# Two-level w_out products spread over 21 steps, three in flight, in eight PSUM banks

## The chip, the cores and the metric

The kernel runs on one core of a Trainium2 chip. A core has a matrix engine (TensorE, PE in the profile, PEld for its weight loads), VectorE (DVE), ScalarE (ACT), GpSimd (POOL) and SyncE (SP), which issues most of the transfers. Each engine works through its own instructions in order; semaphores hold it where it needs what another engine makes. TensorE writes into PSUM, eight banks of 2 KB a partition; VectorE and ScalarE read the banks. The metric is the device time of one execution in microseconds (us), less is better. Before the change the median of three runs is 871.32 us (868.98 to 872.26).

## The reference

The program is an attention block followed by a feed-forward block, all in float32 on the chip (the feed-forward weights arrive as float64).

```python
# attention: q, k, v of shape (8, 12, 448, 64)
scores = norm(q) @ norm(k).T / sqrt(64);  attn = softmax(scores);  x = attn @ v
# bridge to x of shape (3584, 768)
h = x @ w_in                       # w_in 768 x 1024
e = exp(h - max(h));  solu = h * e / (sum(e) + 1e-9)
ln = (solu - mean) / sqrt(var + 1e-6) * g_ln
out = ln @ w_out                   # w_out 1024 x 768
```

## The kernel before

The kernel goes through three stages: attention (to about 332 us of the span), the products with `w_in` (to 585.0 us) and the products with `w_out` (to the end). The diff is about the third.

**Products with fewer multiplications.** Each of the two matrix products is done in Winograd's form of Strassen's scheme: a 2 x 2 block product with 7 block multiplications in place of 8, and sums of blocks ahead and behind. For `w_out` this is done on two levels. The 3584 rows are 7 row blocks (`NS`, index n) of four tiles of 128 rows. For each n there are seven outer products P1 to P7. The outer product of a name takes one wide operand (`HALVES`: a11, a12, s2, s1, s3, s4, a22), made from the transposed activations u, and one of seven prepared weight areas. Inside it are again seven small products, called p1, p2, p6, p5, p7, p4, p3 in their order (`outer_product`, L1152 on). Each is a group of four matmuls of 128 x 128 by 128 x 192 (`mul`, L1158; the matmul is L1168).

**What a group needs and gives.** p1, p6, p7 and p4 add into one bank A, one after the other: after each, the bank is read (`plus`, L1176 on: L1180 on ScalarE for P1 and P5, L1182 on VectorE for the five others, which add a former result at once), and the next group adds into the same bank. So p6 waits for the read after p1, p7 for that after p6, p4 for that after p7. p2 has a bank C, read by VectorE (L1204); p5 and p3 share a bank B, read by VectorE after p7 (L1216, which needs the read of A after p7) and after p3 (L1224). The results of P1, P6 and P7 are kept as Q1, U2 and U3, V is the sum of P6 and P5, and C22 that of P7 and P5 (`finish`, L1235 on, one VectorE instruction of 768 columns each, L1246). Four results of each n are stored by SP (L1231).

**Operands.** u of a tile was written to DRAM in a transposed order by `ff_spread` (a VectorE transpose at L1061, four stores on SP at L1064). `load_u` (L1098) fetches a quarter of 256 KB on SP into a tile called ur. The wide operands come from these: a11, a12, a22 are ScalarE copies (`arrange`, L1116), s1 to s4 VectorE sums (L1121, L1126, L1131, L1136), each made of two instructions (two tiles t) that follow each other. `inner_sums` (L1138) makes the inner block sums with four GpSimd instructions (L1147 to L1150), one of which overwrites a quarter of the operand.

**Order.** The order is written out by hand in slots; a slot holds at most one group. `ORDERS` gives the slot in a period of 49 (one n) at which each outer product begins, and its groups take every second slot from there. So two outer products are in flight, and their groups alternate. `unit` issues the group with all that it entails, and `when(slot, f)` hangs other work behind it: loads, sums, copies. `later(x, f)` runs f when x units have passed; one unit is four slots of this stage, or one product of the stage with `w_in`. So the last tiles' activation work (`ff_max` L1022, `ff_exp` L1028, `ff_mult` L1032, `ff_moments` L1040 on, `ff_norm` L1052, `ff_spread`) runs on inside the first 36 slots of the stage with `w_out`.

**Weight check.** The kernel's float64 conversion holds for weights in a certain range. `check_next` reads both weight matrices again in 28 pieces, every nine slots, and `check_w` (L584) takes the smallest and the largest of each piece with two VectorE reductions (L587, L588); `check_worst` and `check_all` join them with a limit on x into a flag, on which a general path would run instead.

**Memory.** Pools: `big` has tags h, u (three buffers each) and b (two), shared in turn by activations, stores of u and outer results (`big_tile`, L779). For n = 0, a11 and a12 come from a pool `first` ahead of the stage; all others from `u`, opened when the stage begins. PSUM has banks A, B and C for each of two streams and one for the check.

Of the kernel before, what the change touches and what calls it, by code (L numbers as in the profile page):

```python
# [366 lines left out]
def fast_path(  # L367
# [78 lines left out]
    def setup():  # L446
        nc.gpsimd.memset(mhalf, -0.5)
        nc.gpsimd.memset(seven, 7.0)
        nc.gpsimd.memset(eps, 1e-6)


        nc.gpsimd.memset(ones, 0.0)
# [131 lines left out]
    def check_w(x, raw):  # L584

        hi = raw[:, :, 1].bitcast(FP32)
        nc.vector.tensor_reduce(extent[:, 0, x : x + 1], hi, AX, OP.min, apply_absolute_value=True)  # L587
        nc.vector.tensor_reduce(extent[:, 1, x : x + 1], hi, AX, OP.max, apply_absolute_value=True)  # L588

    def check_worst():  # L590
        nc.vector.tensor_reduce(worst[:, 0:1], extent[:, 0], AX, OP.min)
        nc.vector.tensor_reduce(worst[:, 1:2], extent[:, 1], AX, OP.max)
        nc.vector.tensor_reduce(worst[:, 2:3], xmax, AX, OP.max)

    def check_all():
# [3 lines left out]
        pw = last["ps"].tile([P, 4, P], FP32, tag="w", name="pw")[0:1]  # L599
        for i in range(3):  # L600
            nc.tensor.transpose(pw[:, i], worst[:, i : i + 1], ident)
        nc.vector.tensor_reduce(one[:, 0:1], pw[:, 0], AX, OP.min)
        nc.vector.tensor_reduce(one[:, 1:3], pw[:, 1:3], AX, OP.max)
        nc.vector.tensor_scalar(one[:, 0:1], one[:, 0:1], 2.0 ** -15, None, OP.is_ge)
        nc.vector.tensor_scalar(one[:, 1:2], one[:, 1:2], 2.0, None, OP.is_lt)
        nc.vector.tensor_scalar(one[:, 2:3], one[:, 2:3], 256.0, None, OP.is_le)
        nc.vector.tensor_tensor(one[:, 0:1], one[:, 0:1], one[:, 1:2], OP.mult)
        nc.vector.tensor_tensor(one[:, 0:1], one[:, 0:1], one[:, 2:3], OP.mult)
# [489 lines left out]
    def load_u(n, t, h):  # L1098
        own = last.get("u", last["first"])
        r = us[n, "raw", t, h] = own.tile([P, P * HF], FP32, tag="raw", name="ur", bufs=2 if own is last["first"] else 8)  # L1100
# [5 lines left out]
    def operand(n, name):  # L1106
        own = last["first"] if n == 0 and name in ("a11", "a12") else last["u"]
        bufs = 2 if own is last["first"] else 8
        us[n, name] = own.tile([P, 2, HF, 4, 32], FP32, tag="op", name=name, bufs=bufs)
        return us[n, name]  # L1110

    def arrange(n, name, tile, h):

        o = operand(n, name)
        for t in range(2):
            nc.scalar.copy(o[:, t], in_turn(n, tile + t, h))  # L1116

    def sum_s1(n):
        o = operand(n, "s1")
        for t in range(2):  # L1120
            nc.vector.tensor_tensor(o[:, t], in_turn(n, 2 + t, 0), in_turn(n, 2 + t, 1), OP.add)  # L1121

    def sum_s2(n):
        o = operand(n, "s2")
        for t in range(2):
            nc.vector.tensor_tensor(o[:, t], us[n, "s1"][:, t], in_turn(n, t, 0), OP.subtract)  # L1126

    def sum_s3(n):
        o = operand(n, "s3")
        for t in range(2):  # L1130
            nc.vector.tensor_tensor(o[:, t], in_turn(n, t, 0), in_turn(n, 2 + t, 0), OP.subtract)  # L1131

    def sum_s4(n):
        o = operand(n, "s4")
        for t in range(2):
            nc.vector.tensor_tensor(o[:, t], in_turn(n, t, 1), us[n, "s2"][:, t], OP.subtract)  # L1136

    def inner_sums(n, name):  # L1138

        own = last["first"] if n == 0 and name in ("a11", "a12") else last["u"]  # L1140
        a = us[n, name]
        sm = us[n, name, "sums"] = own.tile(
            [P, 3, KC, 4, 32], FP32, tag="sums", name="sums", bufs=2 if own is last["first"] else 4
        )
        a11, a12, a21, a22 = [a[:, t, k * KC : (k + 1) * KC] for t in range(2) for k in range(2)]
        s1, s2, s4 = [sm[:, i] for i in range(3)]
# [5 lines left out]
    def outer_product(n, name, stream):  # L1152
# [5 lines left out]
        def mul(bank, a, i, begin):  # L1158
            x = us[n, operand_name]
            sm = us[n, operand_name, "sums"]  # L1160
            a = {
                "a11": x[:, 0, 0:KC], "a12": x[:, 0, KC:], "s3": x[:, 1, 0:KC], "a22": x[:, 1, KC:],
                "s1": sm[:, 0], "s2": sm[:, 1], "s4": sm[:, 2],
            }[a]
            if begin:
                k[bank] = last["ps"].tile([P, 512], FP32, tag=f"{bank}{stream}", name=bank)[:, 0:N2]
# [24 lines left out]
        def p1():  # L1191
            mul("A", "a11", 0, True)
            us[n, name] = big_tile(name)[:, 0 : 2 * HO].rearrange("p (t n) -> p t n", t=2)
            if name == "P1":
                us[n, "Q1"] = us[n, name]
            if name == "P6":
                us[n, "U2"] = us[n, name]
            if name == "P7":
                us[n, "U3"] = us[n, name]
            plus(temp("q1"), "A", 0, 0)  # L1200

        def p2():
            mul("C", "a12", 1, True)
# [435 lines left out]
```

## Time and profile before

| | before |
|---|---|
| median of 3 runs | 871.32 us |
| profiled execution | 870.22 us |
| its span | 868.3 us |
| TensorE, VectorE busy | 809.5 us, 690.8 us |
| ScalarE, GpSimd busy | 407.2 us, 449.1 us |
| matmuls of the w_out stage | 1372 of 5020 |
| stage with w_out | 585.0 us to the end |

The page is that of one execution. Busy time is the time in which an engine worked on an instruction. A row of a group of instructions has the line, the engine and operation, output and input with shapes, the count, then the busy time and the mean time of one in ns, then the idle time of the engine ahead of them with what ended it. In the table by stage, each row is a stretch of the span, each engine's busy time in it (number of instructions), the granted TensorE clock (1.00 is full), the share of the DMA engines' time and the rate. In a list of waits a row says who waited for whom, the total in us, how many times, and the longest. The chain of waits goes back from the last instruction to what released it; it is given in order of time, with start, length and what ran. The timeline gives start, length and instruction, and in brackets the idle time before it and its releaser.

### The profile page before, as it was taken

The page shows a single profiled execution, that of the slowest core. Times are in us where ns is not written, and L with a number is a line of the kernel's source. Part 1 is how long each engine was busy: PE and PEld are TensorE (multiplying, and loading weights), DVE is VectorE, ACT ScalarE, POOL GpSimd, SP SyncE. Part 2 cuts the span into 40 slices and gives each one's busy share as a digit, 9 for nine tenths or more (in the row PEclk, how much of TensorE's full clock was granted, in tenths as well). Part 3 has the DMA queues.
Part 4 walks back from the last instruction along what each step waited for, and adds up shares of the span by engine and source line. Part 5 has one row for each costly group of instructions (what it writes and reads, how often), then busy time and mean ns, then how long its engine had stood idle before and what let it go on. Part 6 is the DMA issues. An engine that isn't in the chain of part 4 may idle for free. (4 is left out here: it accounts for less than half of the span.)

```text
span 868.3 us, 14895 instructions
## 1 busy us (share of the span) xinstructions
PE 809.5 (93%) x5020; PEld 470.0 (54%) x5020; DVE 690.8 (80%) x1249; ACT 407.2 (47%) x643; POOL 449.1 (52%) x632
## 2 busy tenths in 40 slices
PE   5989999999999999999999999995798978999796
PEld 3334344343444444444444444444797978898796
DVE  5778888887988885899999998886657776776854
ACT  5677876876877862566655544331211102112010
POOL 1343464554564564222444786752755656666560
PEclk9999999999999999999999999997999999999999
DMA  5677877777767634256553454316333625456321
GB/s 115 140 170 180 188 163 176 160 158 176 169 139 173 143 102 123 74 137 191 150 146 86 123 148 118 86 48 193 92 137 126 245 84 191 137 195 218 102 72 60
DMA packets 271941, 122.27 MB, mean 141 GB/s; under 512 B 190704, under 2 KB 257264, under 8 KB 271856
## 3 DMA queue, kind: packets, MB, share of 16 engines
q1 hardware_dynamic: 257600, 111.56, 49.3%
q10 hardware_dynamic: 14256, 9.67, 4.0%
q8 instruction: 42, 0.69, 0.4%
q14 instruction: 43, 0.35, 0.1%
HBM read 84.48 MB, written 36.70 MB: 140 GB/s over the span
## 5 line engine op out<-in xcount | busy, mean ns | idle before, releaser
L968 PE MATMUL b<-w_in,xg 128*128 128x512 f32 x336 | 151.2, 592 | 0.0
L788 ACT ACTIVATE E<-s 128x896 f32<-128x896 f32 x168 | 138.9, 936 | 10.7 <-PE s L798 10.5
L798 PE MATMUL s<-qkT 64*64 64x448 f32 x1152 | 123.1, 554 | 1.4 <-DVE qkT L774 0.8
L968 PE MATMUL b<-w_in,xsum 128*128 128x512 f32 x252 | 115.0, 592 | 0.0
L851 PE MATMUL o<-E,v 128*64 128x448 f32 x576 | 113.5, 543 | 0.0
L968 PEld LDWEIGHTS b<-w_in,xg 128*128 128x128 f32 x336 | 63.8, 190 | 80.2 <-issue 77.4
L670 POOL COPY ss<-part 32x56 f32<-32x56 f32 x88 | 42.0, 477 | 102.7 <-DVE part L660 100.0
L1168 PE MATMUL A<-w_out,s 128*128 128x192 f32 x336 | 69.1, 338 | 23.6 <-DVE u L1182 21.4
L709 POOL TENSOR_TENSOR qkn<-qk,ny 128x896 f32<-128x896 f32 x46 | 77.9, 1713 | 24.1 <-DVE ny L700 10.9
L1168 PE MATMUL B<-w_out,sums 128*128 128x192 f32 x392 | 78.0, 332 | 4.6 <-DVE P L1216 4.6
L798 PEld LDWEIGHTS s<-qkT 64*64 64x64 f32 x1152 | 47.4, 164 | 62.1 <-ACT E L788 30.7
L968 PEld LDWEIGHTS b<-w_in,xsum 128*128 128x128 f32 x252 | 47.9, 190 | 60.3 <-issue 56.4
L851 PEld LDWEIGHTS o<-E,v 128*64 128x64 f32 x576 | 39.2, 137 | 72.6 <-issue 68.0
L1046 POOL TENSOR_TENSOR he<-he,mhalf 128x1 f32<-128x1 f32 x28 | 16.7, 598 | 113.9 <-DVE he L1045 113.5
L1168 PEld LDWEIGHTS A<-w_out,s 128*128 128x128 f32 x336 | 55.4, 191 | 30.8 <-DVE u L1182 23.7
L1168 PEld LDWEIGHTS B<-w_out,sums 128*128 128x128 f32 x392 | 67.4, 194 | 5.1 <-issue 5.1
L1052 ACT ACTIVATE u<-u,shift,he 128x1024 f32<-128x1024 f32 x28 | 34.7, 1239 | 66.8 <-POOL shift L1048 56.5
L1168 PE MATMUL A<-w_out,a 128*128 128x192 f32 x252 | 51.8, 337 | 10.1 <-ACT u L1180 6.0
L660 DVE TENSOR_REDUCE part<-sq 128x28 f32<-128x896 f32 x46 | 49.0, 1082 | 15.2 <-ACT sq L652 13.4
L1147 POOL TENSOR_TENSOR sums<-s 128x256 f32<-128x256 f32 x28 | 21.9, 781 | 70.4 <-PE B L1168 54.9
L1180 ACT COPY q<-A 128x192 f32<-128x192 f32 x14 | 4.5, 318 | 111.0 <-PE A L1168 111.0
L825 DVE TENSOR_TENSOR es<-E 128x896 f32<-128x896 f32 x48 | 52.6, 1097 | 0.5 <-ACT E L788 0.5
(135 smaller groups left out, 1523.4 us busy)
## 6 DMA issues: line engine op xcount, KB each, us to landing
ur<-ud SPq DMA_DIRECT2D x58, 256.0 KB, 4.8
ud<-ub SPq DMA_DIRECT2D x112, 128.0 KB, 2.6
xd<-xo SPq DMA_DIRECT2D x24, 448.0 KB, 3.7
qk<-in_q_dram SPq DMA_DIRECT2D x184, 56.0 KB, 2.3
qk<-in_k_dram SPq DMA_DIRECT2D x184, 56.0 KB, 2.1
v<-in_v_dram SPq DMA_DIRECT2D x24, 384.0 KB, 4.9
out_dram<-P SPq DMA_DIRECT2D x21, 384.0 KB, 2.7
raw<-in_moe_w_in_dram SPq DMA_DIRECT2D x12, 512.0 KB, 4.4
```

The source lines that it names most:

```text
L660: nc.vector.tensor_reduce(norms[m]["part"][:, i], st[n]["sq"], AX, OP.add)
L670: e.tensor_copy(ss[g * 32 : g * 32 + 32], part[o * 32 : o * 32 + 32])
L709: e.tensor_tensor(d["qkn"], d["qk"].rearrange("p s b d -> p (s b) d"), y.rearrange("p b -> p b ()").to_broadcast([P, 2 * NB, 32]), OP.mult,)
L788: nc.scalar.activation(d["E", kc], s[:, :, 0:S], AF.Exp)
L798: nc.tensor.matmul(s[c : c + D, h, 0:S], d["qkT"][hh, 1, keys], d["qkT"][hh, 0, :], start=True, stop=True,)
L825: nc.vector.tensor_tensor(d["es"], d["E", 0], d["E", 1], OP.add)
L851: nc.tensor.matmul(d["o"][h * D : (h + 1) * D, :], quads[n // 2]["v"][:, n % 2 * 2 + h, kc], d["E", kc][:, h], start=False, stop=(kc == NJ ...
L968: nc.tensor.matmul(o, a[:, c], w_in[i][:, c], start=(c == 0), stop=(c == HD - 1))
L1046: nc.gpsimd.tensor_tensor(e, e, mhalf, OP.pow)
L1052: nc.scalar.activation(d["u"], d["u"], AF.Identity, scale=d["e"], bias=d["shift"])
L1147: nc.gpsimd.tensor_tensor(s1, a21, a22, OP.add)
L1168: nc.tensor.matmul(k[bank], a[:, c].rearrange("p a i -> p (a i)"), w_out[:, area, i, c], start=begin and c == 0, stop=c == KC - 1, skip_gr ...
```

## The change

- **Order.** One list `ORDER` = P1, P5, P6, P2, P7, P3, P4 for all n. Outer product number q begins at slot 7q (`STEP`), and its seven groups p1, p2, p6, p5, p7, p4, p3 stand at `PLACES` 0, 4, 8, 10, 12, 16, 20 from there. So three are in flight.
- **PSUM.** A has four banks, B and C two each. The check's bank is gone; it borrows a C bank.
- **Wide sums one by one.** `make(n, name, t)` is one instruction; the two of an operand have slots of their own. s2, s3 and s4 read the copies a11, a12 where they read the loaded tiles before. V and C22 are two instructions of 384 columns each (`both`).
- **First operands.** For n = 0, a11 and s1 (was a12) are made ahead of the stage; the other five are made in slots 0 to 20.
- **Buffers.** Outer results take tags in the order h, u, h, u, h, u, b, b. Loaded quarters have six buffers (was eight), the inner sums have a fourth part in place of the overwrite.
- **Activation work.** `ff_norm` and `ff_spread` of the last two tiles run one unit earlier, `ff_spread` of all others one unit later.
- **Check.** Per piece three ScalarE instructions, three slots apart: two squares with biases and a Relu whose sum goes to `extent`; it is zero if all weights lie in the range. `check_all` takes two transposes in place of three.

```diff
     def check_w(x, raw):
-        hi = raw[:, :, 1].bitcast(FP32)
-        nc.vector.tensor_reduce(extent[:, 0, x : x + 1], hi, AX, OP.min, apply_absolute_value=True)
-        nc.vector.tensor_reduce(extent[:, 1, x : x + 1], hi, AX, OP.max, apply_absolute_value=True)
+        v = raw[:, :, 1]
+        t = last["u"].tile([P, S], FP32, tag="range", name="range", bufs=1)[:, 0 : v.shape[1]]
+        return [
+            lambda: nc.scalar.activation(t, v, AF.Square, scale=2.0 ** -30, bias=limits[:, 0:1]),
+            lambda: nc.scalar.activation(t, t, AF.Square, bias=limits[:, 1:2]),
+            lambda: nc.scalar.activation(t, t, AF.Relu, bias=limits[:, 2:3], accum_out=extent[:, x : x + 1]),
+        ]
...
-            for x, f in zip((1, 2, 3, 5, 7, 9), (ff_max, ff_exp, ff_mult, ff_moments, ff_norm, ff_spread)):
+            waits = (1, 2, 3, 5, 6, 8) if g == NG - 1 else (1, 2, 3, 5, 7, 10)
+            for x, f in zip(waits, (ff_max, ff_exp, ff_mult, ff_moments, ff_norm, ff_spread)):
...
-    ORDERS = (
-        (("P1", 0), ("P2", 9), ("P6", 14), ("P5", 23), ("P7", 28), ("P3", 37), ("P4", 42)),
-        (("P1", 2), ("P5", 7), ("P6", 16), ("P2", 21), ("P7", 30), ("P3", 35), ("P4", 44)),
-    )
-    PERIOD = 49
+    ORDER = ("P1", "P5", "P6", "P2", "P7", "P3", "P4")
+    STEP = 7
+    PLACES = (0, 4, 8, 10, 12, 16, 20)
...
+        if name == "a11":
+            nc.scalar.copy(o, in_turn(n, t, 0))
...
+        elif name == "s1":
+            nc.vector.tensor_tensor(o, in_turn(n, 2 + t, 0), in_turn(n, 2 + t, 1), OP.add)
+        elif name == "s2":
+            nc.vector.tensor_tensor(o, us[n, "s1"][:, t], us[n, "a11"][:, t], OP.subtract)
+        elif name == "s3":
+            nc.vector.tensor_tensor(o, us[n, "a11"][:, t], in_turn(n, 2 + t, 0), OP.subtract)
+        else:
+            nc.vector.tensor_tensor(o, us[n, "a12"][:, t], us[n, "s2"][:, t], OP.subtract)
...
-        nc.gpsimd.tensor_tensor(a21, a11, a21, OP.subtract)
+        nc.gpsimd.tensor_tensor(s3, a11, a21, OP.subtract)
...
-                k[bank] = last["ps"].tile([P, 512], FP32, tag=f"{bank}{stream}", name=bank)[:, 0:N2]
+                tag = f"{bank}{q % 2}" + (str(q // 2 % 2) if bank == "A" else "")
+                k[bank] = last["ps"].tile([P, 512], FP32, tag=tag, name=bank)[:, 0:N2]
...
+    def out_tile(name):
+        tag = "huhuhubb"[len(turns) % 8]
+        turns.append(tag)
...
+        nc.vector.tensor_tensor(us[n, x][:, t], us[n, "U2" if x == "V" else "U3"][:, t], us[n, "P5"][:, t], OP.add)
...
+        follow(parts, 66, lambda: early("a11", 0, (0,)))
+        follow(parts, 67, lambda: early("a11", 1, (0,)))
+        follow(parts, 72, lambda: early("s1", 2, (0, 1)))
+        follow(parts, 77, lambda: early("s1", 3, (0, 1)))
...
+                for place, f in zip(PLACES, outer_product(n, name, q)):
+                    slots[STEP * q + place] = f
...
+                if q > 1:
+                    when(STEP * q - 6, lambda n=n, x=x: inner_sums(n, x))
+            for x, t, slot in (("V", 1, 31), ("V", 0, 34), ("C22", 1, 45), ("C22", 0, 52)):
+                when(base + slot, lambda n=n, x=x, t=t: both(n, x, t))
...
+            at_load = (10, 11, 15, 16, 17, 18, 21, 22) if n == 1 else (4, 5, 8, 9, 10, 11, 16, 17)
+            blocks = (0, 0), (1, 0), (2, 0), (3, 0), (2, 1), (3, 1), (0, 1), (1, 1)
...
+            late = 6 if n == 1 else 0
+            made(n, "a11", base + 12 + late, base + 15 + late)
+            made(n, "s1", base + 21 + late, base + 24 + late)
+            made(n, "s2", base + 28 + late, base + 38)
+            made(n, "a12", base + 33, base + 36)
+            made(n, "s3", base + 40, base + 42)
+            made(n, "s4", base + 47, base + 49)
+            made(n, "a22", base + 53, base + 55)
...
+        made(0, "s2", 0, 3)
+        made(0, "s3", 6, 8)
+        made(0, "a12", 10, 11)
+        made(0, "a22", 12, 14)
+        made(0, "s4", 17, 20)
...
-            when(70 + 9 * x, lambda x=x: check_next(x))
+            when(55 + 9 * x, begin_check)
+            when(58 + 9 * x, go_on)
+            when(61 + 9 * x, go_on)
```

More of the change, by code (lines that the diff above doesn't have):

```diff
@@ L1123, in sum_s2 @@
[L1123 to L1136, printed above, removed]
+        own = last.get("u", last["first"])
@@ L1138, in inner_sums @@
     def inner_sums(n, name):
[L1140 removed]
+        own = last.get("u", last["first"])
         a = us[n, name]
         sm = us[n, name, "sums"] = own.tile(
[L1143 removed]
+            [P, 4, KC, 4, 32], FP32, tag="sums", name="sums", bufs=2 if own is last["first"] else 4
         )
         a11, a12, a21, a22 = [a[:, t, k * KC : (k + 1) * KC] for t in range(2) for k in range(2)]
[L1146 removed]
+        s1, s2, s3, s4 = [sm[:, i] for i in range(4)]
@@ new lines, in fast_path @@
+            for slot, (t, h) in zip(at_load, blocks):
+                when(base + slot, lambda n=n, t=t, h=h: load_u(n, t, h))
+            late = 6 if n == 1 else 0
[6 more added lines that the diff above has]
+            made(n, "a22", base + 53, base + 55)
@@ L1569, in check_first, with begin_check, go_on @@
                 raw[x] = load_again(x)
-        when(60, check_first)
+        when(45, check_first)
         for x in range(len(again)):
-            when(70 + 9 * x, lambda x=x: check_next(x))
-        when(PERIOD * NS - 18, check_worst)
-        when(PERIOD * NS - 12, check_all)
-        for slot in range(PERIOD * NS + 8):
+            def begin_check(x=x):
+                sets["check"] = check_w(x, raw.pop(x))
+                sets["check"].pop(0)()
+            def go_on(x=x):
+                sets["check"].pop(0)()
+                if not sets["check"] and x + 2 < len(again):
+                    raw[x + 2] = load_again(x + 2)
+            when(55 + 9 * x, begin_check)
+            when(58 + 9 * x, go_on)
+            when(61 + 9 * x, go_on)
+        end = period * NS + PLACES[-1] - STEP + 1
+        when(end - 35, check_worst)
+        when(end - 28, check_all)
+        for slot in range(end):
             if slot in slots:
```

146 lines of the change are left out of this document (60 added, 86 removed).

## The prediction

> **What bounds the kernel now.** I read the page first, then the table of busy time by stage, then the chain of waits and the timeline inside the stage that the diff touches.
>
> ```profile
> span 868.3 us, 14895 instructions
> PE 809.5 (93%) x5020; PEld 470.0 (54%) x5020; DVE 690.8 (80%) x1249; ACT 407.2 (47%) x643; POOL 449.1 (52%) x632
> PEclk9999999999999999999999999997999999999999
> ```
>
> TensorE is busy for 93% of the span, which seems to leave little. But the share hides a stage, the w_out products, that starts at 585.0 us, where the one dip of the clock row also lies. By stage (columns: length; busy PE, PEld, DVE, ACT, POOL with counts; clock; DMA share; GB/s; the row with two columns holds the w_out matmuls alone):
>
> ```profile
> 500.00:550.00 50.00, 50.00 (x118) 22.18 (x117) 44.41 (x74) 22.40 (x34) 40.08 (x44) 1.00 0.42 114
> 585.00:645.00 60.00, 43.21 (x215) 40.40 (x216) 39.45 (x79) 11.19 (x23) 28.47 (x38) 0.86 0.40 118
> 645.00:862.50 217.50, 196.35 (x1162) 186.83 (x1160) 153.29 (x367) 30.65 (x76) 120.71 (x155) 1.00 0.45 150
> ...
> 585.00:862.50 277.50, 239.23 (x1372) 227.01 (x1372) 0.97 0.44 143
> ```
>
> 1372 matmuls are 343 groups of four (7 row blocks, 7 outer products, 7 groups). What one group takes undisturbed, and what disturbs it, stands in the chain of waits:
>
> ```profile
> 654.71 0.61 DVE extent L588
> 655.32 1.39 DVE s L1121 x2
> 656.71 0.27 DVE P L1204
> 656.98 0.28 DVE u L1182
> ...
> 657.30 0.92 PE A L1168 x4
> ...
> 660.02 1.19 DVE V L1246
> ...
> 661.53 0.92 PE A L1168 x4
> ...
> 842.38 0.65 PE C L1168 x4
> ```
>
> A group costs 0.65 us, so 343 cost 223 us. The last one ends near 862.2, so the stage takes 277.2 and 54 us of it are waits and slow clock. 54 groups (35 us) fill the first 60 us, 25 over; the other 289 (188 us) fill 217, 29 over. The chain says whom TensorE waits for: VectorE, at a long instruction (a weight check, a wide sum, the sum V) ahead of a short read of a bank. Waits of the steady part, then of the start:
>
> ```profile
> PE A L1168 <- DVE u L1182: 19.6, 19, 1.8
> ...
> PE A L1168 <- ACT u L1180: 6.0, 1, 6.0
> PE B L1168 <- DVE P L1216: 4.6, 1, 4.6
> DVE V L1246 <- DMA ud<-ub: 3.5, 1, 3.5
> ```
>
> **The change, part by part.**
>
> *Three products in flight.* The bank A of a product is read four times between its groups. The shortest such cycle is in the timeline, where a product runs last and alone:
>
> ```profile
> 859.35 0.81 PE L1168 MATMUL A<-w_out,a 128*128 128x192 f32 x4
> ...
> 860.20 0.36 DVE L1182 TENSOR_TENSOR u<-A,P 128x192 f32<-128x192 f32 x1 [0.29 <-PE A L1168]
> ...
> 860.61 0.92 PE L1168 MATMUL A<-w_out,a 128*128 128x192 f32 x4 [0.45 <-DVE u L1182]
> ```
>
> From the start of p7's group to that of p4's: 860.61 - 859.35 = 1.26 us, with VectorE free. Today p7 and p4 stand two slots apart, 1.30 us when another product fills the slot between: 0.04 us to spare, so nearly any VectorE work in the way is paid by TensorE. After, p6, p7 and p4 stand four slots apart (2.60 us): 1.34 us to spare; p1 to p6 and p5 to p3 have eight. The seven places are distinct modulo 7, so from slot 14 every slot holds a group until the last product drains.
>
> *Checks to ScalarE, wide sums one by one.* VectorE's pieces (count, then min/median/max ns in the rows on ur; mean ns in the others):
>
> ```profile
> L1182 DVE TENSOR_TENSOR u<-A,P 128x192 f32<-128x192 f32 x48 | 16.9, 351 | 5.5 <-PE A L1168 5.5
> L587 DVE TENSOR_REDUCE extent<-again 128x1 f32<-128x448 f32 x26 | 15.8, 608 | 0.0
> L1246 DVE TENSOR_TENSOR V<-P,P 128x768 f32<-128x768 f32 x6 | 6.9, 1149 | 0.6
> ...
> L1121 DVE TENSOR_TENSOR s<-ur x14: 679/1196/1235, 592.2 to 804.1; 128x512 f32<-128x512 f32 x14
> L1126 DVE TENSOR_TENSOR s<-s,ur x14: 679/683/686, 595.4 to 816.9; 128x512 f32<-128x512 f32 x14
> L1136 DVE TENSOR_TENSOR s<-ur,s x14: 677/796/1214, 596.6 to 824.4; 128x512 f32<-128x512 f32 x14
> L1131 DVE TENSOR_TENSOR s<-ur x14: 677/684/1215, 600.7 to 819.1; 128x512 f32<-128x512 f32 x14
> ```
>
> The longest single piece falls from a pair (checks, two sums: 1.2 to 2.3 us) to one sum, 0.68 to 1.23 us, or half a V, about 0.57: alone, all below 1.34. A period of 49 slots is 31.9 us. In it VectorE has 41 bank reads (3 for each of P1 and P5, whose other reads are ScalarE's, 7 for each of five others), at the 0.28 that they take back to back in the chain: 11.5. Eight wide sums at the medians: 2 x (1.20 + 0.68 + 0.68 + 0.80) = 6.7. V and C22: 2.3. Together 20.5 us, 64%, where the checks (4 x 1.2) would make it 80%.
>
> What is left is bunching. In slots 38 to 54 stand one s2, two s3, two s4 and two halves of C22: 4.8 us at the medians, 6.7 at the longest, and some 14 reads, 4.0, in 11.05 us. Following the slots one by one, VectorE is at most 0.6 us late at the medians and 1.9 at the longest, so TensorE waits 0 to 0.6 us; for s1, s1, s2, V, V in slots 21 to 34, 0 to 0.4. Loads that come late add something that the rows don't give, 0 to 1 us a period. I take 1 us a period in the middle of these: 6 us for the six steady ones, bounds 0 and 12.
>
> ScalarE gets three instructions for each check. Nearest row, and landings (min/median/max) of the loads ur, then of the check's:
>
> ```profile
> L531 ACT ACTIVATE tmp<-raw,seven 128x384 f32<-128x384 uint32 x16 | 10.2, 637 | 8.4 <-DMA raw<-in_moe_w_out_dram 8.4
> ...
> DMA to landing us min/median/max: 2.6/4.8/6.9
> ...
> DMA to landing us min/median/max: 3.1/3.5/4.6
> ```
>
> Of 448 instead of 384 elements, about 0.7 us each: 28 x 2.1 = 59 us on an engine that was busy 30.65 in 217.5. Its reads for P1 and P5 stand behind single pieces of 0.7 against 1.34 to spare: nothing. Without that cover each check would cost up to 2.1.
>
> *The start.* Waits there were a bank read stuck on ScalarE behind copies whose loads had not landed (6.0), on VectorE behind the same loads (4.6), and V waiting for a buffer that a store held (3.5). The six loads no longer stand behind the stores on SP, the first copies that need them stand at slot 10, and V's buffers come from tags that the stores don't hold: these three go. Two s1 sums move into the stage before; by its row TensorE is busy all the time there and VectorE 44.4 of 50, so they fit (2.4 us if not). What stays is VectorE's own work, now denser:
>
> ```profile
> L1061 DVE STREAM_TRANSPOSE ub<-u 128x1024 f32<-128x1024 f32 x4 | 4.9, 1234 | 2.0 <-DMA ud<-ub 2.0
> L1040 DVE BATCH_NORM_STATS2 bs<-u 128x6 f32<-128x512 f32 x4 | 2.6, 680 | 0.0
> L1032 DVE TENSOR_TENSOR u<-h,u 128x1024 f32<-128x1024 f32 x2 | 2.5, 1236 | 0.0
> ```
>
> Ahead of P1's read at slot 12, VectorE has two s2 (1.4), two transposes (2.5), two products (2.5), two s3 (1.4), one pair of statistics (1.4) and two reads (0.6), and a maximum of about 1.2 left from the stage before: 11 us. P1's p3 at slot 20, 13 groups or 8.5 us in, waits for that read: 2.5 to 4 us. To slot 27 follow two transposes, a second pair of statistics and two s4; from 28 to 48 some 15 us of work stand against 13.7 us of groups. Added up, slot 49 comes 8 us later than its groups alone; bounds 4 (that first wait alone) and 16 (two thirds of today's 25).
>
> ```profile
> 589.50:595.30 5.80, 0.00 (x0) 0.00 (x0) 1.50 (x3) 1.46 (x3) 0.00 (x0) 0.73 0.87 272
> 595.30:609.00 13.70, 9.05 (x27) 8.31 (x28) 13.36 (x26) 1.74 (x3) 6.62 (x8) 0.62 0.61 186
> ...
> 624.20:629.00 4.80, 1.46 (x8) 1.16 (x8) 1.25 (x3) 0.00 (x0) 1.24 (x2) 1.00 0.46 109
> 629.00:632.60 3.60, 3.53 (x13) 3.53 (x14) 3.21 (x9) 0.00 (x0) 0.00 (x0) 0.59 0.01 2
> ```
>
> After the gaps of 5.8 and 4.8 us the granted clock was 0.62 and 0.59. A first wait of 2.5 to 4 us may or may not do it; VectorE would hide most of slow groups, so I add 1 us, bounds 0 and 6. The Trainium skill (TensorE: Matmul & The Clock Gate, "Why this matters for your kernels") sets the limit at idle gaps of about 3 us; the rows agree that 4.8 is over it, and by that rule the term lies nearer 6 than 0 and the time near 836.
>
> *The rest* (an extra sum tile instead of writing in place, one transpose fewer at the end, norms one unit later) is under 0.5 us, hidden behind 0.65 us groups. The drain of the last product: four slots between p7 and p4 hold one group of another, so 0.04 to spare as now: 0.5.
>
> **Sum.** 8 + 1 + 6 + 0.5 = 15.5 of the 54 us stay; 38.5 go. The profiled execution took 870.22 us (span 868.3), 0.13% under the median 871.32: 870.2 - 38.5 = 832.
>
> **Rivals.**
>
> *Loads too late.* s1 follows its loads by 11 slots, 7.2 us, and a11 by 8, 5.2, at landings of 4.8 in the median and 6.9 at most, now with a sixth more traffic per us (277 us of it in 239). If a11 and s1 wait 2 us each period beyond what is spare: 6 x 2 = 12, 844. For it: the small margin; against it: the median.
>
> *VectorE and GpSimd in each other's way.* The sum s1 has 679 and 1235 ns for the same shape. If every wide sum and half V takes the longer time (12 x 0.5 = 6 us a period, VectorE at 83%) about 2.5 us come through: 6 x 2.5 = 15 instead of 6, 841. GpSimd itself, 28 x 0.78 (120.71 by 155) = 22 of 31.9 us, does not bound. The Trainium skill (SBUF — State Buffer, "Who interferes with whom") has a VectorE instruction with two SBUF inputs block, or be blocked by, a GpSimd instruction that reads SBUF, whole; the doubled times agree in kind.
>
> *The start stays as it is* (VectorE bound plus slow clock): 25 instead of 9, 848.
>
> *Nothing gained* (the freed waits fall to another engine at the same rate): about 870. Against it: by the sums above no other engine is busy for over 70% of a period.
>
> *Slower: ScalarE's queue stuck behind the check loads.* A check's first instruction waits for a load issued 12 slots, 7.8 us, before, and bank reads of P1 and P5 (28 of 49 slots) queue behind it. SP holds stores for long:
>
> ```profile
> SPq L1231 <- DVE P L1224: 50.9, 15, 8.9
> ```
>
> Were each load held 8.9 us and landing in 4.6, it would be 5.7 late, 4.4 beyond what is spare, for 16 of the 28 checks: 70 us, 902. It decides from 3.8 us late (16 x 2.4 = 38.5). Against it: what stands before a load on SP was due earlier by its slot, and landings were 3.1 to 4.6.
>
> **Chances.** Forecast 60% (own range 820 to 842), late loads 11%, VectorE against GpSimd 9%, start as it is 8%, nothing gained 4%, slower 6%, and 2% faster than 820. The range 820 to 850 holds the forecast, and the three rivals that end below 850. 0.5%, 4.4 us, is about what can be told from no change here. Faster 0.90, same 0.04, slower 0.06.
>
> **What would show it.** Right: in the steady part TensorE's waits for VectorE under 8 us, not 19.6; groups at 0.65 without the 0.92 restarts; no wait of 4 us or more after the first period; checks on ScalarE and no wait of its bank reads behind them. Wrong: ScalarE or VectorE waiting for ur or the check's tile; a clock well under 1 beyond 610 us; the stage longer than 255 us.

## The result, and the profile after

The median went from 870.15 us (867.11 to 872.26, four runs) to 824.85 us (824.47 to 826.51, four runs): a ratio of 0.9486, with a 95% interval of 0.9452 to 0.9519. The forecast was 832, the range 820 to 850. The profiled execution took 826.51 us. Three rows of its page, which answer to those of before:

```profile
span 824.4 us, 14924 instructions
PE 796.2 (97%) x5019; PEld 465.7 (56%) x5019; DVE 673.0 (82%) x1203; ACT 461.3 (56%) x755; POOL 462.3 (56%) x635
PEclk9999999999999999999999999999999999999999
```

The dip of the clock is gone, and TensorE is busy for 13 us less with the same matmuls (5019 against 5020, as `check_all` has one transpose fewer), none of which runs at a low clock now. By stretches of the stage with w_out (columns as in the prediction):

```profile
586.80:620.00 33.20, 28.04 (x161) 25.93 (x162) 32.58 (x64) 10.02 (x20) 22.63 (x28) 1.00 0.44 134
620.00:818.50 198.50, 197.55 (x1215) 196.76 (x1213) 139.32 (x335) 86.50 (x192) 139.12 (x165) 1.00 0.50 169
```

From 620 us on TensorE is busy 197.55 of 198.50 us. For sizes below a microsecond I use the start of the groups. Here are the first, the 55th, the 155th and the last group after, then three of the same of before (the timeline of TensorE; start, length):

```profile
586.81 0.92 PE L1167 MATMUL A<-w_out,a 128*128 128x192 f32 x4 [0.78 <-DVE h L979]
...
629.00 0.81 PE L1167 MATMUL A<-w_out,sums 128*128 128x192 f32 x4
...
694.00 0.81 PE L1167 MATMUL A<-w_out,s 128*128 128x192 f32 x4
...
817.10 0.81 PE L1167 MATMUL B<-w_out,sums 128*128 128x192 f32 x4
```

```profile
585.01 0.92 PE L1168 MATMUL A<-w_out,a 128*128 128x192 f32 x4 [0.79 <-DVE h L975]
...
645.21 0.81 PE L1168 MATMUL C<-w_out,s 128*128 128x192 f32 x4
...
861.37 0.81 PE L1168 MATMUL B<-w_out,sums 128*128 128x192 f32 x4
```

From 629.00 to 694.00 one hundred groups start, 0.650 us each, without a break. What a stretch takes beyond 0.6505 us a group, I call idle (0.6505 is used for every kernel; with 0.650 each "rest" below would be 0.14 us more). First part, 54 groups: before 60.20 - 35.13 = 25.1 us, after 42.19 - 35.13 = 7.1. Rest, 288 groups: before 216.16 - 187.34 = 28.8, after 188.10 - 187.34 = 0.8. Together 46.1 us went; the stage began 1.8 us later (586.81 against 585.01), and the time from the start of the last group to the end grew by 0.4 us (7.3 against 7.0), so the span is 43.9 us shorter. The 1.8 us can't be told from chance: the first matmul with w_in already starts 1.8 us later (333.41 against 331.61), the diff adds only three small memsets on GpSimd ahead of it, and the kernels of the experiments began the stage anywhere between 584.8 and 589.1 us.

What TensorE, and ScalarE ahead of it, still wait for at the start (584 to 622 us), and in the second fence TensorE's waits from 622 us on; columns: total, times, longest:

```profile
ACT a L1124 <- DMA ur<-ud: 3.0, 2, 2.8
ACT u L1032 <- DVE ub L1065: 2.6, 1, 2.6
PE A L1167 <- ACT u L1179: 2.3, 2, 1.6
...
PE B L1167 <- DVE P L1211: 1.2, 1, 1.2
...
PE A L1167 <- POOL sums L1147: 0.8, 1, 0.8
```

```profile
PE A L1167 <- DVE u L1181: 0.4, 1, 0.4
```

19.6 us in 19 waits for VectorE's bank reads became 0.4 us in one.

### The profile page after: what moved, and what is told of

Read it like the earlier page. It is cut to its first block, busy times and chain, and to the rows that moved or that the text cites. A ratio compares the mean times of both kernels' runs of the same rounds, so it can differ in the third digit from the quotient of the medians.

```text
span 824.4 us, 14924 instructions
## 1 busy us (share of the span) xinstructions
PE 796.2 (97%) x5019; PEld 465.7 (56%) x5019; DVE 673.0 (82%) x1203; ACT 461.3 (56%) x755; POOL 462.3 (56%) x635
## 4 chain that ended last, share of the span: by engine, by line
PE 76%; SPq 9%; DMA 5%; DVE 3%; POOL 3%; ACT 2%; issue 2%; ACTq 0%; DVEq 0%; POOLq 0%
PE b L972 31%; PE A L1167 14%; PE o L855 8%; PE s L802 8%; SPq L634 8%; PE B L1167 7%; PE C L1167 3%; PE sm L874 3%; DMA v<-in_v_dram 2%; PE s L815 1%; PE o L844 1%; DMA qk<-in_k_dram 1%; ACT E L792 1%; DVE part L664 1%; POOL ss L674 1%
## 5 line engine op out<-in xcount | busy, mean ns | idle before, releaser
L1167 PE MATMUL A<-w_out,sums 128*128 128x192 f32 x392 | 80.1, 327 | 3.5 <-ACT u L1179 1.6
L1167 PE MATMUL B<-w_out,sums 128*128 128x192 f32 x392 | 79.9, 326 | 1.2 <-DVE P L1211 1.2
L1167 PEld LDWEIGHTS A<-w_out,sums 128*128 128x128 f32 x392 | 66.0, 190 | 4.9 <-issue 1.8
L563 POOL TENSOR_TENSOR w_out<-w_out 128x384 f32<-128x384 f32 x44 | 50.7, 1158 | 1.9
L656 ACT ACTIVATE sq<-qk 128x896 f32<-128x896 f32 x46 | 43.9, 984 | 13.1 <-DMA qk<-in_k_dram 10.5
L723 DVE STREAM_TRANSPOSE qkT<-qkn 128x896 f32<-128x896 f32 x46 | 48.9, 1094 | 1.9 <-POOL qkn L713 1.8
```

The lines of the kernel that those rows point to most:

```text
L563: nc.gpsimd.tensor_tensor(o, p, q, OP.subtract)
L723: nc.vector.transpose(d["qkT"].rearrange("p s t -> p (s t)"), d["qkn"].rearrange("p b d -> p (b d)"))
L1167: nc.tensor.matmul(k[bank], a[:, c].rearrange("p a i -> p (a i)"), w_out[:, area, i, c], start=begin and c == 0, stop=c == KC - 1, skip_gr ...
```

## The experiments

All are measured beside the kernel before on the same chip; its medians there were 870.9, 871.0 and 873.1 us, so ratios compare better than times where the medians differ. The idle columns are worked out from each kernel's timeline as above. The slots give the order of the groups, so each start in the timeline can be given its name, from p1 to p7. The last column is the part of the idle in the rest by which the groups p4 begin later than 0.6505 us after the group ahead of them.

| kernel | median us | ratio (95%) | idle, first 54 | idle, rest | of it at p4 |
|---|---|---|---|---|---|
| before | 870.2 | | 25.1 | 28.8 | 20.5 |
| after | 824.9 | 0.949 (0.945 to 0.952) | 7.1 | 0.8 | 0.0 |
| e2: before, checks on ScalarE | 863.4 | 0.991 (0.988 to 0.993) | 22.4 | 23.0 | 14.6 |
| e1: after, checks on VectorE | 834.2 | 0.957 (0.954 to 0.961) | 7.1 | 7.6 | 0.3 |
| e4: after, wide sums in pairs | 832.2 | 0.955 (0.952 to 0.957) | 7.5 | 6.1 | 0.0 |
| e3: after, p4 two slots behind p7 | 829.1 | 0.953 (0.949 to 0.956) | 7.5 | 3.1 | 0.0 |
| e8: e1, e3 and e4 in one | 853.2 | 0.979 (0.976 to 0.982) | 8.2 | 24.6 | 12.9 |
| e10: after, six VectorE instructions moved to just ahead of p7 | 827.0 | 0.948 (0.945 to 0.951) | 7.0 | 1.1 | 0.0 |
| e5: the same, p4 three slots behind p7 | 830.9 | 0.952 (0.949 to 0.954) | 8.8 | 2.7 | 0.2 |
| e9: the same, p4 two slots behind p7 | 836.9 | 0.960 (0.958 to 0.963) | 8.4 | 10.5 | 6.5 |
| e11: after, two products in flight | 837.8 | 0.960 (0.957 to 0.962) | 10.0 | 11.1 | 8.1 |
| e6: after, first loads behind the stores | 830.3 | 0.953 (0.950 to 0.956) | 11.5 | 0.8 | 0.0 |
| e7: after, transposes earlier | 829.4 | 0.951 (0.948 to 0.953) | 9.8 | 0.8 | 0.0 |
| e12: after, two VectorE instructions left out | 823.9 | 0.943 (0.941 to 0.946) | 4.4 | 0.8 | 0.0 |

My theory was the prediction's: a bank of A must be read between p7 and p4, that cycle had 0.04 us to spare and has 1.34, and VectorE's longest pieces are now shorter than that. The rivals were that VectorE's load as such decided, that only one part of the change carries the gain, and, for the start, that the loads or VectorE's work bound it.

**e1 and e2: the checks alone.** e1 puts the two reductions back into the new order; e2 moves them to ScalarE in the old one.

```diff
-        v = raw[:, :, 1]
...
-            lambda: nc.scalar.activation(t, t, AF.Relu, bias=limits[:, 2:3], accum_out=extent[:, x : x + 1]),
+        hi = raw[:, :, 1].bitcast(FP32)
+        nc.vector.tensor_reduce(extent[:, 0, x : x + 1], hi, AX, OP.min, apply_absolute_value=True)
+        nc.vector.tensor_reduce(extent[:, 1, x : x + 1], hi, AX, OP.max, apply_absolute_value=True)
...
-            when(55 + 9 * x, begin_check)
-            when(58 + 9 * x, go_on)
-            when(61 + 9 * x, go_on)
+            when(58 + 9 * x, check_next)
```

> The changed kernel with the 28 weight checks back on VectorE as two reductions each (about 1.1 us together); all else stays. Theory of the spare time (the reads of a bank now have 1.34 us to spare in place of 0.04, so pieces under that are hidden): TensorE's waits for VectorE in the steady part stay under 5 us and the time comes to 825 to 830 us. Rival, VectorE's load (the gain came from taking 30 us of checks off VectorE): the waits return to about 20 us, 840 to 846 us.

```diff
-            when(70 + 9 * x, lambda x=x: check_next(x))
+            when(67 + 9 * x, begin_check)
+            when(70 + 9 * x, go_on)
+            when(73 + 9 * x, go_on)
```

> The kernel before with this one part of the change alone: the checks as three ScalarE instructions, two products in flight as before. Theory of the spare time: only what waits behind a check goes, by the chain of waits some 5 to 8 us: 862 to 866 us. Rival, VectorE's load: most of the 20 us of the steady part goes, 850 to 855 us.

Undoing the checks costs 834.2 - 824.9 = 9 us, of which 6.9 are idle in the rest and 1.2 come behind the last group. That lies between the two expectations (825 to 830 by the spare time, 840 to 846 by VectorE's load), so the spare time of 1.34 us did not hide a check of two reductions, 1.2 us, wherever it stood. The lateness is not at p4: p7, which waits for the read of A after p6, has 3.6 us of it, and p5, whose bank B was used by an earlier product, has 2.3. Moving the checks alone (e2) came out inside the range of the spare time, 862 to 866. It gains 7.5 us, 5.8 of the idle in the rest and 2.7 at the start. The waits of e2 from 622 us on show what was left over; from 644 us on, where the rest begins, they are 14.5 us in 20:

```profile
PE A L1170 <- DVE u L1184: 18.9, 21, 3.2
```

Taking the checks off VectorE is worth a sixth of the gain when it is done alone, and p4 still begins late by 14.6 us. The cost of the checks on ScalarE came as costed, 62.2 us for 28 of them against 59 (line, operation, shapes, count; busy us, mean ns; idle before):

```profile
L593 ACT ACTIVATE range<-again,limits 128x448 f32<-128x448 uint32 (+1 forms) x28 | 19.8, 706 | 1.8 <-DMA again<-in_moe_w_out_dram 1.2 <-DMA again<-in_moe_w_in_dram 0.3
L594 ACT ACTIVATE range<-range,limits 128x448 f32<-128x448 f32 (+1 forms) x28 | 18.6, 663 | 0.3
L595 ACT ACTIVATE range<-range,limits 128x448 f32<-128x448 f32 (+1 forms) x28 | 18.5, 662 | 0.4
...
L595 ACT ACTIVATION_READ_ACCUMULATOR range<-range,limits 128x1 f32 x28 | 5.3, 189 | 0.0
```

The wait for the check's loads, the mechanism of the rival at 902 us, was 1.5 us in all 28.

**e4, e3 and e8: pairs, the close p4, and three parts undone at once.**

```diff
-            for x, t, slot in (("V", 1, 31), ("V", 0, 34), ("C22", 1, 45), ("C22", 0, 52)):
+            for x, t, slot in (("V", 1, 34), ("V", 0, 34), ("C22", 1, 52), ("C22", 0, 52)):
...
-            made(n, "s1", base + 21 + late, base + 24 + late)
-            made(n, "s2", base + 28 + late, base + 38)
+            made(n, "s1", base + 24 + late, base + 24 + late)
+            made(n, "s2", base + 38, base + 38)
```

and s3, s4 and the operands of n = 0 likewise in e4; in e3 one line,

```diff
-    PLACES = (0, 4, 8, 10, 12, 16, 20)
+    PLACES = (2, 4, 8, 10, 12, 14, 20)
```

and in e8 the edits of e1, e3 and e4 together.

> The changed kernel with the two instructions of each wide sum s1 to s4, of V and of C22 at one slot (the later of the two), one behind the other as before. Theory of the spare time: pieces of 1.2 to 2.4 us against 1.34 to spare, so four of the six pairs of a period cost 0 to 1 us each, 829 to 837 us. Rival, VectorE's load, which does not change: 825 us, within 2.

> The changed kernel with the seven places 2, 4, 8, 10, 12, 14, 20 in place of 0, 4, 8, 10, 12, 16, 20: p4 comes two slots after p7, as in the kernel before, so that this one read has 0.04 us to spare; three products stay in flight and VectorE's work is the same. Theory of the spare time: waits of A's p4 for VectorE come back, 8 to 14 us in the steady part, 833 to 839 us. Rival, VectorE's load: 825 us, within 2.

> The changed kernel with three parts undone at once: the checks on VectorE, the sums in pairs, and p4 two slots after p7. Each alone left TensorE 6.9, 5.4 and 2.3 us more idle beyond the first 54 groups (0.75 us in the changed kernel, 28.8 in the one before). Theory of separate costs: they add up, 15 us there, about 840 us. Theory of one shared reserve (each part uses up the same spare time, so that together they cost more than their sum): 20 to 29 us there, 845 to 854 us.

e4 came out as the spare time expected (829 to 837), but at p7 and not at p4: its groups p7 are late by 5.2 us, most of it in one place a period. e3 missed both expectations: with the old 0.04 us to spare only 2.3 us of idle came back, and p4 is not late at all. What came back are 0.07 us each at 29 groups p6, which stand right behind a p4. Alone, the parts cost 6.9 (checks), 5.4 (pairs) and 2.3 (close p4) in the rest, 14.6 in sum; together they cost 24.6 - 0.8 = 23.8. That is what a shared reserve expected (20 to 29), not separate costs (15): while two of the three are in place they cover a part of what the third would have covered. Most of the surplus stands at p4, which is late by 0.3, 0.0 and 0.0 us in the three kernels alone and by 12.9 in e8; p7 has another 7.2 there. What e8 keeps (the order with three in flight, banks, buffers, first operands and loads) gains 28.8 - 24.6 = 4.2 us in the rest by itself, but 25.1 - 8.2 = 17 at the start: nearly the whole gain there. e8's waits for VectorE come near those of before (19.6 us in 19):

```profile
PE A L1167 <- DVE u L1181: 14.1, 19, 1.7
```

**e9, e10 and e5: why e3 cost so little.** p7 stands at slots 5, 12, 19, 26, 33, 40 and 47 of a period, and the changed order has no piece of VectorE longer than a read directly ahead of one of them. So I moved six VectorE instructions there (one of s1, one of s2, both of s4, half of V and half of C22; the expectations count s4 once), with p4 as changed (e10), three slots behind p7, 3 x 0.65 - 1.26 = 0.69 us to spare (e5), and two slots behind (e9). In e5 p7 stands three slots behind p6 as well, so that cycle has 0.69 us in place of 1.34 too.

```diff
-            for x, t, slot in (("V", 1, 31), ("V", 0, 34), ("C22", 1, 45), ("C22", 0, 52)):
+            for x, t, slot in (("V", 1, 32), ("V", 0, 34), ("C22", 1, 46), ("C22", 0, 52)):
...
-            made(n, "s1", base + 21 + late, base + 24 + late)
-            made(n, "s2", base + 28 + late, base + 38)
+            made(n, "s1", base + 21 + late, base + 25 + late)
+            made(n, "s2", base + 28 + late, base + 39)
...
-            made(n, "s4", base + 47, base + 49)
+            made(n, "s4", base + 46, base + 53)
```

with PLACES of e3 in e9 and `(0, 4, 9, 10, 12, 15, 20)` in e5.

> The changed kernel with p4 two slots after p7, and besides with five VectorE pieces of each period (second s1, first V half, second s2, first C22 half, both s4) moved by one to four slots, into the slot right ahead of a p7. Theory of place: p4 at two slots cost only 2 to 4 us because no long piece stood right ahead of a p7; now each piece delays that read by 0.3 to 0.9 us with 0.04 to spare, 8 to 18 us beyond the first 54 groups, 833 to 842 us. Rival (two slots are enough wherever the pieces stand): 829 us, within 2.

> The same five pieces right ahead of a p7, with the places of the changed kernel (p4 four slots after p7). Theory of the spare time: 1.34 us hide a piece of 0.6 to 1.2 us, 825 to 827 us. Rival (the place of the pieces counts by itself): as much slower as with p4 close, 833 us and more.

> The five pieces right ahead of a p7 once more, now with p7 three slots after p6 and p4 three after p7 (places 0, 4, 9, 10, 12, 15, 20): 0.69 us to spare, between the 1.34 and the 0.04 of the two runs before, which idled 1.06 and 10.5 us beyond the first 54 groups. Theory of the spare time: 2 to 5 us there, 827 to 831 us. Rival (a step: anything over two slots hides all): about 1 us, 825 to 827 us.

With the same pieces at the same slots, 0.04, 0.69 and 1.34 us to spare left 10.5, 2.7 and 1.1 us of idle in the rest; all three came out inside what the spare time expected. Of that, p4 is late by 6.5, 0.2 and 0.0 us; in e9 another 3.5 stand at the p6 right behind, and in e5 more stands at p7 (1.3 us, 0.5 in e10) than at p4. So the shorter the spare time, the more is paid, and the step between 0.04 and 0.69 us is the large one. It says what e3 had missed: the place of the pieces, not their number, makes the reserve needed. e9's stretch from 620 us on, beside e3's in the next fence, rules out VectorE's load once more:

```profile
620.00:818.50 198.50, 194.79 (x1155) 186.13 (x1155) 124.86 (x316) 86.15 (x192) 125.48 (x165) 1.00 0.49 164
```

```profile
620.00:818.50 198.50, 198.21 (x1206) 194.09 (x1204) 130.99 (x330) 86.17 (x192) 139.42 (x164) 1.00 0.48 164
```

VectorE is busy 0.108 us a matmul in e9 (124.86 by 1155) and 0.109 in e3, less than the 0.115 after (139.32 by 1215), and TensorE idles more.

**e11: two products in flight**, with eight banks, single sums and the checks on ScalarE as changed.

```diff
-                for place, f in zip(PLACES, outer_product(n, name, q)):
-                    assert STEP * q + place not in slots
-                    slots[STEP * q + place] = f
+                first = base + ((0, 9, 14, 23, 28, 37, 42), (2, 7, 16, 21, 30, 35, 44))[n % 2][i]
+                for k, f in enumerate(outer_product(n, name, q)):
+                    assert first + 2 * k not in slots
+                    slots[first + 2 * k] = f
```

> The changed kernel with two outer products in flight, in the slots of the kernel before (begins 0, 9, 14, 23, 28, 37, 42 and 2, 7, 16, 21, 30, 35, 44, a group every second slot); checks on ScalarE, single sums, buffers, first loads and eight banks stay as changed (the second C22 half comes two slots earlier, so that its buffers allow it). Theory of the spare time: p7 to p4 has 0.04 us to spare, p5 to p3 about 1, and the single pieces stand at places that suit other slots: 4 to 12 us of idle TensorE beyond the first 54 groups in place of 0.75, 829 to 838 us. Rival (short pieces off VectorE are all that counts, three in flight nothing): 825 to 827 us. A start as before (25 us) would add to either.

e11 came out as expected: 11.1 us of idle instead of 0.8 in the rest, in many short waits (15 for VectorE, 0.5 us at most), and 8.1 of it at p4, which stands two slots behind p7 again. With the short pieces of the change, the third product in flight is worth up to 10 us there and 2.9 at the start; up to, since the pieces kept places that were chosen for three in flight. With the long pieces and the close p4 of before the third one brought at most the 4.2 us of e8: short pieces, spare time and the third product appear to be worth more together than apart.

**e6 and e7: the first loads.** e6 issues the six loads after the stores of the last tiles. e7 was meant as an improvement: the transposes of most tiles two units earlier, the statistics of the last two one unit later, to thin VectorE's work at the start.

```diff
-        for h in range(2):
-            for t in (2, 3):
-                load_u(0, t, h)
-        for t in range(2):
-            load_u(0, t, 1)
+        for t, h in ((2, 0), (3, 0), (2, 1), (3, 1), (0, 1), (1, 1)):
+            when(4, lambda t=t, h=h: load_u(0, t, h))
```

```diff
-            waits = (1, 2, 3, 5, 6, 8) if g == NG - 1 else (1, 2, 3, 5, 7, 10)
+            waits = (1, 2, 3, 6, 7, 8) if g == NG - 1 else (1, 2, 3, 5, 7, 8)
```

> The changed kernel with the six loads of the first row block hung behind slot 4, so that they stand on SP behind the stores of the transposed tiles, as in the kernel before. Theory of the loads: ScalarE's copies and VectorE's s3 wait for them as before, the first 54 groups lose 6 to 12 us more than the 7 us of now, perhaps with a slow clock: 831 to 838 us. Rival (the start is bound by VectorE's own work, which covers the loads): 825 to 827 us.

> The changed kernel with the transposes of all tiles but the last two run two units earlier (8 in place of 10 after their product), so that the two that fell in the first slots fall ahead of the stage, and the statistics of the last two tiles one unit later. Theory (VectorE's work bounds the start): VectorE idles about 1.6 us just ahead of the stage, so up to 2.4 us of transposes leave the start: 822 to 824 us. Rival (the work comes to stand ahead of the last reads of the stage before): 825 to 827 us.

Both issue the loads late and both lose: 4.4 us of idle in e6, 2.7 in e7, all at the start. e6 lost less than the theory of the loads expected (6 to 12 us, 831 to 838) and more than its rival did. e7 missed both of its expectations (822 to 824, 825 to 827): that its stores would hold the loads on SP was in neither. When SP issues them (start, length, queue) after, in e6 and in e7, where SP stood 22.7 us at the stores that wait for the moved transposes:

```profile
577.09 2.80 SPq L1104 DMA_DIRECT2D ur<-ud  x6
```

```profile
592.17 2.79 SPq L1104 DMA_DIRECT2D ur<-ud  x6
```

```profile
567.04 22.72 SPq L1068 DMA_DIRECT2D ud<-ub  x16
589.87 15.73 SPq L1104 DMA_DIRECT2D ur<-ud  x14
```

And e6's ScalarE and TensorE (timeline): a read of bank A is held behind a copy whose load has not landed, and after the gap a group takes 1.65 us.

```profile
598.20 1.22 ACT L1124 COPY a<-ur 128x512 f32<-128x512 f32 x2 [6.25 <-DMA ur<-ud]
599.33 0.31 ACT L1179 COPY u<-A 128x192 f32<-128x192 f32 x1
```

```profile
599.69 1.65 PE L1167 MATMUL A<-w_out,a 128*128 128x192 f32 x4 [5.41 <-ACT u L1179]
```

It is the 6.0 us wait of before come back. It accounts for 4.4 of the 18 us that the start gained. How the other 13.6 divide among V's buffers, the operand made ahead, the order and the slow groups wasn't tried.

**e12: what bounds the start that is left.**

```diff
-        nc.vector.tensor_tensor(d["u"], d.pop("h"), d["u"], OP.mult)
+        h = d.pop("h")
+        if t < NT - 2:
+            nc.vector.tensor_tensor(d["u"], h, d["u"], OP.mult)
```

> The changed kernel without the product of h and the exponentials (128 x 1024, VectorE, 1.2 us each) for the last two tiles, so that VectorE has 2.5 us less to do in the first slots; the output of these two tiles is then another. Theory (the start is bound by VectorE's own work): the 7 us of idle TensorE in the first 54 groups become 4 to 5, 822 to 823 us. Rival (it is bound by waits of ScalarE and GpSimd for each other): no change, 825 us.

2.5 us less work for VectorE, 2.7 us less idle for TensorE, as the theory of VectorE's work expected; the time, 823.9, lies 0.9 us above its range. So 2.7 of the 7.1 us at the start hang on VectorE's own work, which the first row of stretches after suggests too (busy 32.58 of 33.20 us). Of the 4.4 us left in e12, TensorE waits 1.6 for a bank read of ScalarE and 1.4 for GpSimd's sums; they were not taken apart further. No version that does the whole work beat the changed kernel.

## Why the prediction was right, step by step

- **The mechanism held.** TensorE paid for VectorE's long pieces ahead of a bank read; with 1.34 us to spare it no longer does. Its tests came out: waits for VectorE 0.4 us (under 8 was asked for), groups at 0.65, no wait of 4 us or more, the stage about 231 us where over 255 would have spoken against it. By groups, p4 was late by 20.5 of the 28.8 us of the rest before, and by nothing after. Two signs did not come out clean: ScalarE did wait for ur at the start (3.0 us), and three of its 56 bank reads began 0.2 to 0.7 us late behind a check, with no wait of TensorE. And the size of the pieces alone doesn't tell what 1.34 us hides: with two reductions (1.2 us) or two sums in a row, e1 and e4 still cost 6.9 and 5.4 us, at p7 and p5. The prediction's list of cycles also left one out: bank B goes from the p3 of a product to the p5 of the next but one, four slots later, and there e1's p5 waits. (The eight slots that it gives from p5 to p3 are those from p7, after which B is read; from p5 to p3 it is ten.)
- **The term for the steady part was mis-sized**: 6 us (bounds 0 to 12), measured 0.8. The step that failed is "I take 1 us a period in the middle of these". My slot-by-slot count gave 0 to 0.6 and 0 to 0.4 us a period; I then added 0 to 1 for late loads, which no row gave. The nearest rows, landings of 4.8 us at the median against leads of 5.2 and 7.2, spoke for 0 (the longest, 6.9, for a little); after, the loads landed in 4.1 us at the median and 6.4 at most, and ScalarE waited for ur at the start only. That is most of the 7 us between forecast and result.
- **The slow clock**: 1 us, measured 0, its lower bound. The granted clock was 1.00 in both stretches. The row that I called a gap of 4.8 us (624.20 to 629.00) is none: it holds 1.46 us of matmuls, and the longest gap there was 3.41 us, so it doesn't show that 4.8 us is too long. The longest wait of TensorE at the start was 1.55 us after. That the clock stayed full was in part luck: in e9 and e11 it fell with gaps no longer than that (last section).
- **The start**: 8 us, measured 7.1, but made up otherwise. The wait that I put first, P1's p3 at slot 20, came where predicted (B for P at L1211) with 1.2 us, not 2.5 to 4. About as much came from what I had not seen: ScalarE's bank read stood behind an exponential that waited 2.6 us for a transpose of VectorE, and TensorE waited 0.8 us and less for GpSimd's inner sums.
- **The drain**: 0.5, measured 0.07 over the last six groups.
- **The sum**: 15.5 us should stay and 38.5 go; 7.8 stayed, and 46 went in the stage.
- **"So they fit"** for the two sums moved into the stage before held: from 500 to 550 us VectorE rose from 44.41 to 47.72 of 50 us, TensorE stayed at 50.00 of 50, and from the first matmul with w_in to the first with w_out it is 253.4 us in both.
- **VectorE's share** was put at 64% of a period and measured 70% (139.32 of 198.50). That fits the rival "VectorE and GpSimd in each other's way", which was half right: the pieces did grow (half of V took 0.91 us in the mean and half of C22 0.77 in place of 0.57; the last section has more), but the reserve hid it.
- **The other rivals** left no trace in the steady part. Late loads came at the start alone (3.0 us for ur), and the check's loads held ScalarE for 1.5 us in all.
- **The parts were not priced one by one** in the sum, and could not have been: by e1, e4, e3 and e8 the single prices (6.9, 5.4, 2.3) don't add up to that of the three.

## What to carry to other kernels

Where a bank is filled, read and filled again, count what that cycle has to spare in the order of the work, and hold the longest piece of the reading engine against it, and against the slots at which the pieces stand: here 0.04, 0.69 and 1.34 us to spare cost 10.5, 2.7 and 1.1 us for the same pieces. Do so for each such cycle: once p4 had room, what was left stood at p7 and p5. Several small measures can draw on one reserve, so undo them together before you value them one by one. At the border of two stages look at the order within each queue: loads issued late behind stores on SP, with a bank read queued on ScalarE behind the copy that needs them, cost 4.4 and 2.7 us of idle here.

## What the runs showed of the hardware

**The same sum takes one or two lengths.** Half of V, or of C22, of one shape (ns, minimum, median and maximum over 14), and two cases from the timeline, with GpSimd beside it:

```profile
L1241 DVE TENSOR_TENSOR V<-P,P x14: 557/907/1079, 610.5 to 803.8; 128x384 f32<-128x384 f32 x14
L1241 DVE TENSOR_TENSOR C<-P,P x14: 547/554/1123, 619.9 to 814.9; 128x384 f32<-128x384 f32 x14
```

```profile
642.28 0.73 POOL L1148 TENSOR_TENSOR sums<-s,sums 128x256 f32<-128x256 f32 x1
642.37 1.06 DVE L1241 TENSOR_TENSOR V<-P,P 128x384 f32<-128x384 f32 x1
...
655.55 0.55 DVE L1241 TENSOR_TENSOR C<-P,P 128x384 f32<-128x384 f32 x1
655.65 1.04 POOL L1147 TENSOR_TENSOR sums<-s 128x256 f32<-128x256 f32 x1
```

Whichever came second took longer: V 1.06 us where GpSimd had begun first, GpSimd 1.04 where VectorE had. The last two halves of C22 (811.12 and 814.90 us) ran with no GpSimd instruction beside them and took 0.56 and 0.55 us. The Trainium skill (SBUF — State Buffer, "Who interferes with whom") calls the port that the two share an exclusive lock; these rows agree.

**The clock fell after short gaps too.** In e9 no gap at the start was longer than 1.25 us, and in e11 none longer than 1.49; still the granted clock went to half. e9's TensorE (timeline), then two stretches of e11:

```profile
592.33 0.89 PE L1167 MATMUL A<-w_out,sums 128*128 128x192 f32 x4 [1.25 <-ACT u L1179]
593.72 1.25 PE L1167 MATMUL A<-w_out,a 128*128 128x192 f32 x4 [0.50 <-ACT u L1179]
594.76 1.49 PE L1167 MATMUL A<-w_out,sums 128*128 128x192 f32 x4
```

```profile
596.00:600.00 4.00, 1.59 (x6) 1.33 (x7) 3.73 (x15) 1.96 (x3) 1.36 (x4) 0.84 0.96 323
600.00:604.00 4.00, 4.00 (x14) 4.00 (x14) 2.06 (x4) 2.58 (x4) 3.92 (x6) 0.50 0.44 136
```

In e11 TensorE had been busy 1.59 of 4 us, over several gaps. The records of the clock say more than single gaps do. In each of the 14 traces the granted clock changes only at multiples of 3.41 us from one of its changes, so each trace can be laid out in stretches of 3.41 us. Two of e9, then two of the changed kernel, the first with most of its gap of 1.55 us:

```profile
590.74:594.16 3.42, 1.68 (x10) 1.12 (x9) 3.42 (x3) 3.42 (x8) 2.97 (x3) 1.00 0.58 153
594.16:597.57 3.41, 3.41 (x12) 3.41 (x12) 3.31 (x7) 1.18 (x4) 0.00 (x0) 0.50 0.64 157
```

```profile
589.02:592.43 3.41, 1.96 (x13) 1.66 (x11) 3.41 (x5) 1.71 (x5) 2.99 (x3) 1.00 0.22 56
592.43:595.85 3.42, 3.32 (x20) 3.35 (x21) 3.42 (x4) 2.61 (x6) 1.27 (x2) 1.00 0.52 140
```

TensorE was busy for 0.49 of the first stretch in e9, and the next had half the clock; in the changed kernel it was 0.57, and the clock stayed full. From 25 us to the last group the 14 traces have 3259 stretches at full clock. All 19 in which TensorE was busy for less than 0.45 of the time were followed by half the clock, of the ten from 0.45 to 0.50 two were, and of all others none. Half the clock then lasted one or two stretches. So in these traces it is the busy share of such a stretch that goes with the slow clock, and a gap counts by how much of a stretch it takes. This was found by sorting the stretches afterwards; no run was made to test it.

The prediction went by single gaps, and by the Trainium skill's limit of about 3 us (TensorE: Matmul & The Clock Gate, "Why this matters for your kernels"); here gaps half as long were enough when they came close together in one stretch.
